# A new order of all steps and transfers in a one-core attention and gated-convolution kernel

## The chip, the cores and the metric

The kernel runs on one core of a Trainium2 chip. A core has five engines that run side by side, each through its own queue of instructions and strictly in the order of that queue as far as this kernel's rows show: PE (TensorE, matmuls; its weight loads are shown apart as PEld), DVE (VectorE), ACT (ScalarE), POOL (GpSimd) and SP (SyncE, which here only issues transfers). Matmul results land in PSUM; the other data lie in SBUF. POOL has no access to PSUM in this program: whatever it works on was first copied out by ACT or DVE. The metric is the device time of one execution in microseconds (us); lower is better.

## What is computed

Eight batches, eight heads, 576 rows. In each head the rows of k and v are first pooled into 32 slots with softmax weights made from phi, then each row of q attends to the 32 slots. The heads side by side are x (8, 576, 512), which goes through a causal convolution of five taps with a sigmoid (the gate) and through two matrix products:

```python
a = softmax(phi, axis=2)                        # per slot over the 576 rows
k_m = einsum('bhsm,bhsd->bhmd', a, k);  v_m = einsum('bhsm,bhsd->bhmd', a, v)
attn = softmax(q @ k_m.T / sqrt(64));   x = attn @ v_m      # heads side by side
gate_pre[:, s] = sum_k conv_w[k] * x[:, s - 4 + k]
out = (sigmoid(gate_pre) * (x @ w_val)) @ w_out
```

The weights arrive as float64 and are narrowed to float32 on the chip; the last products are made of a high and a low part each (three matmuls for one), so that they are exact enough.

## The kernel before

The program is cut into 900 small steps. A step is a function such as `project(k, i)`; its arguments are batch, half, group or tile. A string, `ORDER` (lines 41 to 143), names every step once, and a loop at the end calls them in that order. Each engine's queue is filled in the order in which the string reaches its instructions, so `ORDER` fixes the order on all five engines, the transfers on SP among them; semaphores between the engines follow from which step reads what another wrote. A star behind a name moves the step's work to its second engine (`pick(usual, other)`).

The steps of one batch, with the line by which the profile knows them:

- `load_phi`, `load_kv`, `load_rest`, `load_q` (L229 to L244) and, once, `load_w` (L258): transfers in, all issued by SP. The weights' transfers share two buffers (`hH`), so a later one waits until an earlier one was narrowed (`narrow_size` L267, `narrow_bits` L272, `narrow_round` L280, `narrow_add` L286, `narrow_done` L295, on ACT, DVE and POOL).
- `phi_max`, `phi_turn`, `phi_top`, `phi_spread`, `phi_sub` (L378: POOL, starred DVE), `phi_exp`: the first softmax.
- `slots` (PE L392, 40 matmuls in the trace), `slots_inv`, `slots_scale`, `slots_turn` (L422), `slots_place`, `scores` (PE L442), `scores_turn` (DVE L454), the `soft_...` steps (`soft_inv` begins on DVE L507, starred on ACT L505; `soft_high` is a copy, `soft_low` a subtraction).
- `val_rows` (PE L542) and `val_copy`, `val_high`, `val_low`: x @ w_val is made through the slots.
- the gate: for batch 0 `conv` (PE L580) and `sigmoid`; for the others `mix` (PE L593), which puts attn @ v_m into a PSUM tile `cv`, then five `tap` steps for each of two groups of channels. `tap.b.s.g.0` is on ACT: it reads `cv` and writes `gate` (two instructions, L615). Starred, it also writes the fifth tap into a tile `part` (two more of L615). Taps 1 to 4 are on DVE (two instructions each, L617, which read `cv` and `gate`); in a starred group the fifth is instead added by POOL from `part` (L609). `open_gate` is the sigmoid (ACT L622).
- `value` (PE L637), `gated` (DVE L650; starred a copy on ACT L648 and the product on POOL L650), `gated_high` (a copy, L209) and `gated_low` (a subtraction, L212: POOL, starred DVE).
- for each pair of batches, nine tiles of rows: `project` (PE L675, 12 matmuls), `place` (L209: PSUM to SBUF on ACT, starred on DVE), `store` (SP L685).

All copies have line L209 and all subtractions of low parts L212. PSUM holds two kinds of tiles: `b`, four buffers, shared by all small products, `value` and `project`; and `cv`, two buffers. `part` has one buffer. `warm` (PE L219) are matmuls whose result nobody reads.

```python
    def pick(usual, other):
        return other if live["other"] else usual
        ...
    with tc.manual_schedule():
        for x in ORDER.split():
            name, *args = x.rstrip("*").split(".")
            live["other"] = x.endswith("*")
            steps[name](*(int(a) if a.isdigit() else a for a in args))
```

Of the kernel before, what the change touches and what calls it, by code (L numbers as in the profile page):

```python
# [46 lines left out]
phi_lay.1 narrow_done.v.2 spread_taps.0 warm.2 narrow_bits.v.3 phi_exp.0.1 load_w.o.3 narrow_add.v.0 phi_sub.1*
slots_inv.0.0 narrow_done.v.0 slots_scale.0.0* narrow_add.v.3 slots.0.1 narrow_done.v.3 place_taps.0 load_rest.1
narrow_size.v.1 slots_inv.0.1 narrow_round.v.1 narrow_bits.v.1 slots_scale.0.1 narrow_add.v.1 slots_turn.0 taps.0.0*
narrow_done.v.1 spread_taps.1 phi_exp.1 slots_place.0 load_w.o.0 load_kv.1.1 scores.0 scores_turn.0.0 narrow_size.o.3  # L50
load_w.o.1 narrow_bits.o.3 soft_max.0.0 scores_turn.0.1 soft_sub.0.0* load_kv.1.0 place_taps.1 narrow_size.o.0
taps.0.1 val_rows.0 load_w.o.2 val_copy.0.1 soft_exp.0.0 soft_max.0.1 val_high.0.1 soft_sum.0.0 narrow_round.o.3
soft_inv.0.0 load_phi.2 warm.8 soft_sub.0.1 val_copy.0.0 soft_exp.0.1 val_high.0.0 soft_mul.0.0* narrow_round.o.0
slots.1.1 soft_turn.0.0 soft_high.0.0 slots_inv.1.1 turn_taps.0 soft_sum.0.1 narrow_add.o.3 conv.0.0 narrow_size.o.1
load_rest.2 narrow_done.o.3 sigmoid.0.0.1 sigmoid.0.0.0 narrow_size.o.2 soft_inv.0.1 soft_mul.0.1* val_low.0.1
narrow_round.o.1 soft_turn.0.1 narrow_bits.o.1 load_q.1 val_low.0.0 soft_low.0.0 slots.1.0 narrow_round.o.2
narrow_bits.o.0 narrow_bits.o.2 phi_max.2 conv.0.1 slots_scale.1.1* slots_inv.1.0 load_phi.3 soft_high.0.1 phi_turn.2
phi_top.2 narrow_add.o.1 value.0.0.1 narrow_done.o.1 narrow_add.o.2 slots_scale.1.0* sigmoid.0.1.0 lay_taps.0
phi_spread.2 slots_turn.1 phi_lay.2 slots_place.1 value.0.0.0 gated.0.0.1 load_kv.2.0 scores.1.0 sigmoid.0.1.1
scores.1.1 wo_high.1 narrow_add.o.0 val_rows.1 narrow_done.o.2 value.0.0.3 phi_sub.2 phi_exp.2 wo_high.3 val_copy.1.1  # L60
warm.2 gated.0.0.0 scores_turn.1.0 load_kv.2.1 scores_turn.1.1 wo_high.2 soft_max.1 gated.0.0.3 value.0.0.2
soft_low.0.1 soft_sub.1 phi_max.3 value.0.1.0 slots.2.0 gated.0.1.0 load_kv.3.0 narrow_done.o.0 phi_turn.3 wo_low.2
value.0.1.1 gated.0.0.2 slots_inv.2.0 val_copy.1.0 slots.2.1 soft_exp.1 gated_high.0.0.1 wo_low.1 value.0.1.2
soft_sum.1 gated_high.0.0.0 gated_low.0.0.1 phi_top.3 load_q.2 wo_low.3 gated.0.1.1 soft_inv.1* slots_scale.2.0*
phi_spread.3 slots_inv.2.1 wo_high.0 slots_scale.2.1* slots_turn.2 value.0.1.3 wo_low.0 soft_mul.1* load_phi.4
val_high.1.1 gated.0.1.2 phi_lay.3 soft_turn.1 slots_place.2 val_rows.2 gated_high.0.1.0 mix.1.1 gated_low.0.0.0
project.0.1 load_rest.3 phi_max.4 gated.0.1.3* project.0.0 val_high.1.0 val_low.1.1 tap.1.1.0.0 soft_high.1
tap.1.1.1.0* val_low.1.0 tap.1.1.0.1 tap.1.1.0.2 scores.2.0 tap.1.1.0.3 scores.2.1 soft_low.1 tap.1.1.1.1 tap.1.1.1.2
tap.1.1.1.3 gated_high.0.1.1 tap.1.1.1.4 tap.1.1.0.4 gated_low.0.1.1 scores_turn.2.0 scores_turn.2.1 value.1.1.3
val_copy.2.0 place.0.1 load_q.3 gated_low.0.1.0 soft_max.2 open_gate.1.1.0 mix.1.0 phi_turn.4 value.1.1.2 soft_sub.2  # L70
store.0.1 place.0.0 val_copy.2.1 value.1.1.1 load_kv.3.1 open_gate.1.1.1 tap.1.0.1.0* phi_sub.3 project.0.2
gated.1.1.3 tap.1.0.0.0 soft_exp.2 phi_top.4 gated.1.1.2 tap.1.0.1.1 place.0.2 phi_spread.4 load_phi.5 phi_exp.3
tap.1.0.1.2 project.0.3 val_high.2.1 value.1.0.2 tap.1.0.1.3 phi_lay.4 slots.3.0 tap.1.0.0.1 load_kv.4.0 soft_sum.2
soft_inv.2 tap.1.0.1.4 tap.1.0.0.2 place.0.3 tap.1.0.0.3 soft_mul.2 gated_high.1.1.1 tap.1.0.0.4 soft_turn.2 slots.3.1
mix.2.1 open_gate.1.0.1 tap.2.1.0.0 value.1.1.0 phi_sub.4 slots_inv.3.0 gated.1.1.1 load_rest.4 store.0.0 value.1.0.3
gated_low.1.1.1 slots_inv.3.1 gated.1.1.0* gated.1.0.2 value.1.0.0 slots_scale.3.0 slots_scale.3.1* load_kv.4.1
# [665 lines left out]
```

## Time and profile before

| | |
|---|---|
| time, median of 3 runs | 262.78 us (262.44 to 268.13) |
| the profiled execution's own time | 262.44 us |
| its span, first to last instruction | 260.6 us |
| time outside the span | 1.84 us (262.44 less 260.6) |
| granted TensorE clock, mean | 0.987 |
| bytes read and written | 37.92 MB and 9.44 MB |

The span is made of a head of some 40 us, in which data arrive and the weights are narrowed, a long middle in which PE, DVE, ACT and POOL work on several batches at once, and an end of some 15 us in which PE multiplies the last tiles by w_out. In the rows below a line is one group of instructions, with its busy time, the mean of one, and, behind the second bar or in brackets, how long the engine sat idle before them and what ended that.

### The profile page before, as it was taken

To read this page: it belongs to the slowest core of one execution; us is meant where nothing else is said; L and a number is where in the kernel's file an instruction comes from. 1 tells how busy PE (TensorE), PEld (TensorE's weight loads), DVE (VectorE), ACT (ScalarE), POOL (GpSimd) and SP (SyncE) were. 2 spreads that over 40 slices of the span, in tenths; PEclk is the share of its full clock that TensorE was granted. 3 is DMA by queue.
4 is the path that set the end of the run, shared out by engine and by line. 5 is a ranking of instruction groups with operands and counts; after the bars stand their busy time and mean duration, and the time that the engine had idled before them with its cause. 6 is when DMAs were issued, how large, how long until landed. Compare 5 with 4: busy or idle time off the path is not lost.

```text
span 260.6 us, 5969 instructions
## 1 busy us (share of the span) xinstructions
PE 234.0 (90%) x2344; PEld 180.2 (69%) x2344; DVE 214.7 (82%) x411; ACT 176.5 (68%) x328; POOL 181.8 (70%) x134
## 2 busy tenths in 40 slices
PE   1288889899999999999999999999987999999995
PEld 0255578574587777786868578866766587978884
DVE  2486898899999998899898999869679889799510
ACT  2454769877897978877878889477773595950402
POOL 2271485999999999877979799977495778840300
PEclk9999779999999999999999999999999999999999
DMA  6999995972191989803953009814501202122114
GB/s 187 402 358 334 401 396 155 394 291 89 21 361 50 384 282 346 298 9 123 390 221 121 3 3 337 330 42 114 190 3 40 76 11 111 53 80 82 40 47 154
DMA packets 12571, 47.73 MB, mean 183 GB/s; under 512 B 1400, under 2 KB 1656, under 8 KB 9600
## 3 DMA queue, kind: packets, MB, share of 16 engines
q1 hardware_dynamic: 12544, 47.36, 49.4%
q8 instruction: 18, 0.29, 0.5%
q14 instruction: 9, 0.07, 0.1%
HBM read 37.92 MB, written 9.44 MB: 182 GB/s over the span
## 4 chain that ended last, share of the span: by engine, by line
PE 34%; DVE 22%; DMA 14%; ACT 13%; POOL 11%; issue 4%; SPq 1%; ACTq 0%; DVEq 0%; POOLq 0%
PE b L675 17%; DVE gate L617 9%; PE b L637 8%; DMA out_dram<-o 8%; DMA hH<-in_w_val_dram 4%; ACT gate L615 3%; DMA hH<-in_w_out_dram 2%; PE cv L593 2%; POOL e L378 2%; POOL h L650 2%; PE cv L442 2%; POOL gate L609 2%; ACT part L615 2%; DVE ss L498 2%; PE b L392 2%
## 5 line engine op out<-in xcount | busy, mean ns | idle before, releaser
L617 DVE SCALAR_TENSOR_TENSOR gate<-cv,cwP,gate 128x288 f32<-128x288 f32 x202 | 88.6, 505 | 10.2 <-ACT part L615 6.2
L675 PE MATMUL b<-woH,hL 128*128 128x512 f32 (+1 forms) x148 | 58.1, 393 | 0.6 <-DVE ri L399 0.4
L675 PE MATMUL b<-woH,hH 128*128 128x512 f32 (+1 forms) x148 | 57.0, 385 | 0.0
L675 PE MATMUL b<-woL,hH 128*128 128x512 f32 (+1 forms) x148 | 56.8, 384 | 0.0
L650 POOL TENSOR_TENSOR h<-h,gate 128x288 f32<-128x288 f32 x30 | 26.8, 904 | 20.0 <-ACT h L648 14.8
L212 POOL TENSOR_TENSOR hL<-h,hH 128x576 fp32r<-128x576 f32 x25 | 35.6, 1429 | 5.8 <-ACT hH L209 4.3
L675 PEld LDWEIGHTS b<-woH,hL 128*128 128x128 f32 x148 | 27.8, 188 | 7.3 <-issue 1.6
L637 PE MATMUL b<-pL,vwH 128*128 128x288 f32 x128 | 29.7, 313 | 2.9 <-ACT vwF L209 1.2
L675 PEld LDWEIGHTS b<-woH,hH 128*128 128x128 f32 x148 | 27.8, 188 | 5.7
L675 PEld LDWEIGHTS b<-woL,hH 128*128 128x128 f32 x148 | 27.8, 188 | 4.9
L209 ACT COPY o<-b 128x512 f32<-128x512 f32 (+1 forms) x28 | 16.0, 579 | 21.1 <-PE b L675 21.0
L615 ACT ACTIVATE gate<-cv,cwP 128x288 f32<-128x288 f32 x56 | 24.6, 507 | 5.3 <-PE cv L593 4.9
L622 ACT ACTIVATE gate<-gate 128x576 f32<-128x576 f32 x28 | 19.1, 689 | 12.9 <-DVE gate L617 7.2
L637 PE MATMUL b<-pH,vwH 128*128 128x288 f32 x128 | 27.4, 295 | 0.0
L637 PE MATMUL b<-pH,vwL 128*128 128x288 f32 x128 | 27.3, 295 | 0.0
L637 PEld LDWEIGHTS b<-pL,vwH 128*128 128x128 f32 x128 | 20.5, 189 | 9.5 <-issue 3.5
L286 POOL TENSOR_TENSOR hL<-hL 128x512 int32<-128x512 int32 (+1 forms) x9 | 13.4, 1507 | 18.3 <-ACT hL L280 13.2
L209 ACT CAST hH<-h 128x576 fp32r<-128x576 f32 x26 | 17.6, 681 | 7.8 <-DVE h L650 4.6
L212 POOL TENSOR_TENSOR pL<-pT,pH 128x1152 fp32r<-128x1152 f32 (+1 forms) x9 | 22.5, 2501 | 0.0
L392 PE MATMUL b<-kv,e 128*32 128x129 f32 x512 | 19.3, 295 | 1.6 <-DMA kv<-in_kv_dram 1.3
L609 POOL TENSOR_TENSOR gate<-gate,part 128x576 f32<-128x576 f32 x11 | 16.3, 1478 | 6.1 <-DVE gate L617 4.9
L637 PEld LDWEIGHTS b<-pH,vwL 128*128 128x128 f32 x128 | 20.5, 188 | 0.0
(90 smaller groups left out, 466.7 us busy)
## 6 DMA issues: line engine op xcount, KB each, us to landing
kv<-in_kv_dram SPq DMA_DIRECT2D x16, 1032.0 KB, 9.1
out_dram<-o SPq DMA_DIRECT2D x35, 256.0 KB, 2.5
q<-in_q_dram SPq DMA_DIRECT2D x7, 1152.0 KB, 6.3
e<-in_phi_dram SPq DMA_DIRECT2D x7, 640.0 KB, 6.6
rest<-in_rest_dram SPq DMA_DIRECT2D x8, 258.0 KB, 7.9
...
```

The source lines that it names most:

```text
L209: eng.copy(out=out, in_=x) if eng is nc.scalar else eng.tensor_copy(out=out, in_=x)
L212: eng.tensor_tensor(out=out, in0=x, in1=hi.bitcast(F32), op=ALU.subtract)
L286: nc.gpsimd.tensor_tensor(out=a, in0=a, in1=r, op=ALU.add)
L378: eng.tensor_tensor(out=t, in0=t, in1=mxa.unsqueeze(3).to_broadcast(list(t.shape)), op=ALU.subtract)
L392: nc.tensor.matmul(km[j * M:(j + 1) * M, 0:2 * D + 1], lhsT=e[:, g, j * M:(j + 1) * M, c], rhs=x[:, c, j, :] if c < C - 1 else rests[b % 2 ...
L609: nc.gpsimd.tensor_tensor(out=gt, in0=gt, in1=part, op=ALU.add)
L615: nc.scalar.activation(out=o[:, t], in_=x, func=AF.Identity, scale=w)
L617: nc.vector.scalar_tensor_tensor(out=o[:, t], in0=x, scalar=w, in1=o[:, t], op0=ALU.mult, op1=ALU.add)
L622: nc.scalar.activation(out=gt, in_=gt, func=AF.Sigmoid)
L637: nc.tensor.matmul(vp[:, 0:HALF], lhsT=a[:, t // PG, n:n + P], rhs=p[:, g, s * HALF:(s + 1) * HALF], start=(i == 0), stop=(i == len(parts) ...
L650: eng.tensor_tensor(out=h[:, i], in0=x, in1=gt, op=ALU.mult)
L675: nc.tensor.matmul(ps, lhsT=h, rhs=w, start=(n == 0), stop=(n == len(parts) - 1))
```

## The change

`ORDER` is replaced. The same 900 steps stand in it, each once, in another sequence; nothing else of the kernel differs. A line of it before and one after, at the same place in the work (the first half of batch 5's gate):

```diff
-tap.5.1.1.4 tap.5.0.0.0* gated_low.4.1.1* project.2.0 val_low.5.1 value.5.1.0 tap.5.0.0.1 tap.5.0.0.2 open_gate.5.1.0
...
+phi_spread.7 value.5.1.0 gated.4.0.1* tap.5.1.0.3 gated_high.4.0.0 tap.5.1.1.4 tap.5.0.0.0 value.5.1.1 place.1.5*
+slots_place.6 gated_low.4.0.0 tap.5.0.1.0* load_q.6 tap.5.1.0.4 gated_low.4.1.1 project.2.0 scores.6.0 place.1.6*
+open_gate.5.1.0 tap.5.0.0.1 tap.5.0.0.2 val_rows.6 gated_low.4.1.0 tap.5.0.0.3 store.1.2 gated.5.1.1* scores.6.1
```

Stars differ too, so some work changes its engine. Counted over the string, DVE loses three `gated_low`, three `place`, one `phi_sub`, four first halves of `soft_inv` and one fifth tap, and gains two `soft_low`, one `soft_high` and one `taps`; one `gated` leaves it and one `gated_high` comes to it. POOL gains the three `gated_low`, the `phi_sub` and the fifth tap's addition and loses the two `soft_low`. ACT gains the three `place`, and its queue holds 18 loads of an activation table where it held 16.

The head, on PE. Rows of PE's queue from batch 0's slots (L392, from `kv` and `rest`) to its scores (L442); L302 spreads the convolution weights, L219 are the warming matmuls. Before:

```order
L392 MATMUL b<-kv_78,e 32x129 x16
L392 MATMUL b<-rest_81,e 32x129 x4
L302 MATMUL b<-taps,kvT 128x320
L219 MATMUL cv<-ident 128x128 x2
L392 MATMUL b<-kv_79,e 32x129 x16
L392 MATMUL b<-rest_81,e 32x129 x4
L422 MATMUL b<-ident,kvd 128x128 x3
L302 MATMUL b<-taps,kvT 128x320
L442 MATMUL cv<-q,kvT 32x288 x16
```

Of the change, on PE, from the same slots:

```order
L392 MATMUL b<-kv_78,e 32x129 x16
L392 MATMUL b<-rest_81,e 32x129 x4
L392 MATMUL b<-kv_79,e 32x129 x16
L392 MATMUL b<-rest_81,e 32x129 x4
L365 MATMUL b<-ident,top 128x128 x2
L422 MATMUL b<-ident,kvd 128x128 x3
L442 MATMUL cv<-q,kvT 32x288 x16
```

The second group's slots now follow the first's directly: the weight spreading and the warming matmuls went ahead of both. On SP, the transfer of `rest` now stands ahead of that of `kv_78`, not behind it.

The middle, on DVE. Rows of DVE's queue at the first half of batch 5: before, `gate_2245<-cv_2213` is the group whose first taps on ACT also write `part`, and `gate_2290<-cv_2214` the other; `hL_708` is a `gated_low`. Before:

```order
L212 TENSOR_TENSOR hL_708<-h_2128,hH_694 128x2x288
L617 SCALAR_TENSOR_TENSOR gate_2245<-cv_2213,cwP_84,gate_2245 128x288 x6
L209 COPY o_2334<-b_2252 128x512
L454 STREAM_TRANSPOSE st_2336<-cv_2281 128x576
L617 SCALAR_TENSOR_TENSOR gate_2290<-cv_2214,cwP_84,gate_2290 128x288 x2
```

Of the change, on DVE, at the same half; here `gate_2251<-cv_2202` is the group without `part`, and `gate_2266<-cv_2203` the one with it:

```order
L209 COPY o_2298<-b_2176 128x512
L617 SCALAR_TENSOR_TENSOR gate_2251<-cv_2202,cwP_84,gate_2251 128x288 x8
L650 TENSOR_TENSOR h_2319<-b_2237,gate_2169 128x288
L454 STREAM_TRANSPOSE st_2336<-cv_2289 128x576
L617 SCALAR_TENSOR_TENSOR gate_2266<-cv_2203,cwP_84,gate_2266 128x288 x2
L454 STREAM_TRANSPOSE st_2336<-cv_2322 128x576
```

DVE now takes the group without `part` first, all four of its taps, and comes to the group with `part` two steps after that.

The evictions, on ACT. Rows of ACT's queue where tiles of the first pair of batches leave PSUM (`o<-b` is a `place`); `e` is `phi_exp`, `st` is `soft_exp`, `gate<-gate` is `open_gate`. Before:

```order
L383 ACTIVATE e_743<-e_743 128x1280
L209 COPY o_1214<-b_1164 128x512
L209 CAST vwH_1232<-vwF_1184 128x512
L209 CAST hH_706<-h_1130 128x2x288
L492 ACTIVATE st_1162<-st_1162 128x1152
```

Of the change, on ACT, from the same `phi_exp` on; `b_1169` is `project.0.7`, which was the first of the three to be multiplied:

```order
L383 ACTIVATE e_652<-e_652 128x1280
L209 COPY o_1288<-b_1214 128x512
L209 COPY vwF_1290<-b_1142 128x512
L209 CAST vwH_1295<-vwF_1199 128x512
L492 ACTIVATE st_1184<-st_1184 128x1152
L615 ACTIVATE gate_1299<-cv_1270,cwP_84 128x288 x2
L411 ACTIVATE kvd_1285<-b_1248,ri_1292 128x128
L411 ACTIVATE kvd_1285<-b_1248,ri_1292 128x64
L622 ACT_TABLE_LOAD
L622 ACTIVATE gate_1077<-gate_1077 128x576
L209 COPY o_1361<-b_1317 128x512
L209 COPY o_1370<-b_1169 128x512
```

Tile 0.7 (`b_1164` before, `b_1169` now) left right behind the `phi_exp`; now 0.8 and 0.5 leave ahead of it, with a softmax, first taps, a table load and an `open_gate` between.

## Rows read from the trace of the kernel before

**Rows 1.** Page, busy time and share of the span of each engine.

```profile
PE 234.0 (90%) x2344; PEld 180.2 (69%) x2344; DVE 214.7 (82%) x411; ACT 176.5 (68%) x328; POOL 181.8 (70%) x134
```

**Rows 2.** Page, chain that ended last, share of the span by engine.

```profile
PE 34%; DVE 22%; DMA 14%; ACT 13%; POOL 11%; issue 4%; SPq 1%; ACTq 0%; DVEq 0%; POOLq 0%
```

**Rows 3.** Windows: busy us per engine, clock, DMA share, GB/s; the long middle.

```profile
60.00:240.00 180.00, 172.88 (x1629) 133.05 (x1629) 163.06 (x327) 134.08 (x250) 144.30 (x99) 1.00 0.41 147
```

**Rows 4.** Timeline of PE in the head: start, us, line, [idle <-releaser].

```profile
15.07 1.95 PE L392 MATMUL b<-kv,e 128*32 128x129 f32 x32 [0.20 <-DMA kv<-in_kv_dram]
...
17.38 1.43 PE L302 MATMUL b<-taps,kvT 8*128 8x320 f32 x2
...
19.90 1.95 PE L392 MATMUL b<-kv,e 128*32 128x129 f32 x32
...
34.83 4.48 PE L580 MATMUL cv<-pT,taps 32*64 32x288 f32 x80 [1.16 <-DVE ri L399]
```

**Rows 5.** Windows, the stretch in which the second `kv` arrives.

```profile
10.00:20.00 10.00, 7.59 (x60) 5.35 (x64) 7.93 (x15) 6.96 (x14) 6.64 (x4) 1.00 0.99 383
```

**Rows 6.** Page, issues of two transfers: count, KB each, median us to landing.

```profile
kv<-in_kv_dram SPq DMA_DIRECT2D x16, 1032.0 KB, 9.1
...
rest<-in_rest_dram SPq DMA_DIRECT2D x8, 258.0 KB, 7.9
```

**Rows 7.** Waits of DVE, 43 to 245 us: us in total, times, longest.

```profile
DVE gate L617 <- ACT part L615: 6.2, 5, 2.2
...
DVE gate L617 <- ACT gate L615: 3.7, 5, 1.6
```

**Rows 8.** Timeline of ACT, first half of batch 5's gate.

```profile
171.23 0.91 ACT L615 ACTIVATE gate<-cv,cwP 128x288 f32<-128x288 f32 x2
172.67 0.90 ACT L615 ACTIVATE part<-cv,cwP 128x288 f32<-128x288 f32 x2 [0.53 <-POOL gate L609]
```

**Rows 9.** Timeline of DVE at the same place.

```profile
173.60 2.64 DVE L617 SCALAR_TENSOR_TENSOR gate<-cv,cwP,gate 128x288 f32<-128x288 f32 x6 [2.24 <-ACT part L615]
```

**Rows 10.** Groups of DVE by form: count, busy us, mean ns.

```profile
L617 DVE SCALAR_TENSOR_TENSOR gate<-cv,cwP,gate 128x288 f32<-128x288 f32 x202 | 88.6, 505 | 10.2 <-ACT part L615 6.2 <-ACT gate L615 3.7
L212 DVE TENSOR_TENSOR hL<-h,hH 128x576 fp32r<-128x576 f32 x7 | 5.9, 849 | 0.8 <-ACT hH L209 0.7
L209 DVE COPY o<-b 128x512 f32<-128x512 f32 x8 | 5.5, 687 | 7.1 <-DMA out_dram<-o 3.8 <-PE b L675 3.1
L507 DVE TENSOR_SCALAR ss<-ss 128x36 f32<-128x36 f32 x6 | 3.7, 621 | 0.1
L378 DVE TENSOR_TENSOR e<-e,mxa 128x1280 f32<-128x1280 f32 x1 | 1.5, 1473 | 0.0
L209 DVE CAST pH<-pT 128x1152 fp32r<-128x1152 f32 x2 | 2.1, 1038 | 0.0
L567 DVE TENSOR_TENSOR taps<-h,kvd 128x320 f32<-128x320 f32 x1 | 1.4, 1412 | 0.0
L212 DVE TENSOR_TENSOR vwL<-vwF,vwH 128x512 fp32r<-128x512 f32 x2 | 4.4, 2214 | 0.0
```

**Rows 11.** Groups of POOL and ACT by form that the moved work joins or leaves.

```profile
L212 POOL TENSOR_TENSOR hL<-h,hH 128x576 fp32r<-128x576 f32 x25 | 35.6, 1429 | 5.8 <-ACT hH L209 4.3 <-DVE hH L209 1.4
L212 POOL TENSOR_TENSOR pL<-pT,pH 128x1152 fp32r<-128x1152 f32 x7 | 19.2, 2747 | 0.0
L609 POOL TENSOR_TENSOR gate<-gate,part 128x576 f32<-128x576 f32 x11 | 16.3, 1478 | 6.1 <-DVE gate L617 4.9 <-ACT gate L622 1.2
L378 POOL TENSOR_TENSOR e<-e,mxa 128x1280 f32<-128x1280 f32 x6 | 15.2, 2538 | 1.7 <-ACT mxa L209 1.7
L209 ACT COPY o<-b 128x512 f32<-128x512 f32 x27 | 15.6, 586 | 19.3 <-PE b L675 19.3
L622 ACT ACT_TABLE_LOAD x7 | 9.0, 1283 | 0.1
```

**Rows 12.** Waits of ACT, 43 to 245 us: us in total, times, longest.

```profile
ACT gate L622 <- POOL gate L609: 5.6, 1, 5.6
```

More of the change, by code (lines that the diff above doesn't have):

```diff
@@ L47 @@
[L47 to L76, printed above, removed]
@@ L137 @@
[L137 to L141 removed]
+load_w.c.0 load_phi.0.0 load_w.v.3 load_phi.0.1 narrow_size.c.0 narrow_round.v.3 narrow_round.c.0 phi_max.0.0
@@ new lines @@
+open_gate.1.0.0 value.1.0.0 slots_place.3 value.1.0.3 gated.1.0.1* gated_high.1.1.0 tap.2.1.0.4 gated_low.1.1.0
+gated.1.0.0 gated.1.0.2* store.0.2 tap.2.1.1.0* val_rows.3 gated.1.0.3* phi_sub.4 gated_high.1.0.0 phi_max.5
+scores.3.0 tap.2.1.1.1 project.0.7 store.0.3 gated_high.1.0.1 scores_turn.3.0 val_low.2.0 soft_high.2* scores.3.1
+val_copy.3.1 load_q.4 scores_turn.3.1 phi_turn.5 phi_exp.4 soft_max.3 phi_top.5 tap.2.1.1.2 project.0.8 slots.4.0
+slots.4.1 gated_low.1.0.1 mix.2.0 tap.2.1.1.3 slots_inv.4.0 slots_scale.4.0 place.0.8 val_copy.3.0 slots_inv.4.1
@@ new lines @@
+val_high.3.1 soft_sub.3 soft_exp.3 tap.2.0.0.0 soft_low.2* tap.2.0.0.1 load_kv.5.0 soft_sum.3 load_rest.5 phi_spread.5
+slots_scale.4.1* gated_low.1.0.0 open_gate.2.1.0 project.0.5 project.0.6 project.0.4 soft_inv.3 val_low.3.1
+tap.2.1.1.4 place.0.5 tap.2.0.0.2 load_phi.6 soft_mul.3 tap.2.0.0.3 place.0.7 load_kv.5.1 val_high.3.0 phi_lay.5
+tap.2.0.0.4 open_gate.2.1.1 tap.2.0.1.0* soft_turn.3 value.2.1.3 open_gate.2.0.0 phi_sub.5 store.0.5 place.0.6
+value.2.0.1 tap.2.0.1.1 value.2.0.0 tap.2.0.1.2 tap.2.0.1.3 phi_exp.5 gated.2.1.3 mix.3.1 slots.5.1 slots.5.0
@@ new lines @@
+tap.5.0.1.2 gated.5.0.0* tap.5.0.1.3 value.5.1.3 soft_sub.6 gated.5.1.2 soft_exp.6 gated.5.1.3 soft_sum.6 phi_exp.7
+project.2.2 value.5.0.3 soft_inv.6 slots.7.1 store.1.5 gated_high.5.1.1 soft_mul.6* soft_turn.6 slots_inv.7.1
+tap.5.0.1.4 open_gate.5.0.1 slots.7.0 mix.6.1 place.2.1 value.5.0.1 place.2.2 val_high.6.0 gated_low.5.1.0*
+val_low.6.1 tap.6.1.0.0 slots_inv.7.0 slots_scale.7.1* tap.6.1.1.0* store.1.4 load_q.7 gated.5.0.3* slots_scale.7.0
+soft_high.6 tap.6.1.0.1 value.5.0.2 tap.6.1.0.2 project.2.3 slots_turn.7 gated.5.0.1 gated_low.5.1.1* place.2.3
@@ new lines @@
+project.2.4 tap.6.0.0.2 gated.6.1.3 tap.6.0.0.3 store.2.1 project.2.8 soft_sum.7 tap.6.0.0.4 val_low.7.0 soft_inv.7
+gated_high.6.1.0 gated_high.6.1.1 place.2.8* tap.6.0.1.2 soft_mul.7 project.2.5 value.6.0.1 value.6.0.2
+gated_low.6.1.1 tap.6.0.1.3 gated_low.6.1.0 tap.6.0.1.4 project.2.6 place.2.4 soft_turn.7 open_gate.6.0.0 mix.7.0
+value.6.0.0 soft_high.7* gated.6.0.1 val_low.7.1 soft_low.7* open_gate.6.0.1 gated.6.0.2* tap.7.0.0.0 place.2.6*
+gated.6.0.0* tap.7.0.0.1 value.6.0.3 tap.7.0.0.2 store.2.3 tap.7.0.1.0* project.3.3 store.2.7 gated_high.6.0.0
```

145 lines of the change are left out of this document (76 added, 69 removed).

## Prediction

> **What bounds the kernel now.** I read the page's busy shares first [rows 1]: PE is busy 90% of the 260.6 us, DVE 82%, POOL 70%, ACT 68%. No engine stands far apart, so a single bound is not to be expected. The chain that ended last says the same [rows 2]: followed back from the end it runs 34% of the span through PE, 22% through DVE, 14% through transfers, 13% through ACT and 11% through POOL. The windows then show where PE has room [rows 3]: between 60 and 240 us it is busy 172.88 of 180 us, which leaves 7.1 us, while DVE is busy 163.06 and so idles 16.9 us, ACT 45.9, POOL 35.7. The rest of PE's idle time lies in the head. So an order can gain in two ways: by making the head shorter, and by taking from the middle waits that keep PE from work. The work itself hardly changes: the matmuls are the same in number.
>
> Next come DVE's own waits in the middle [rows 7]. The largest is for ACT's first taps: 6.2 us in five waits behind the writing of `part`, and 3.7 us in five behind the writing of `gate`. What such a wait is shows in batch 5 [rows 8, 9]. ACT has written `gate` by 172.14 (171.23 + 0.91), which is all of ACT's data that DVE's second tap reads. It then waits 0.53 us for POOL to give back the one `part` buffer and writes `part` until 173.57. DVE starts at 173.60, 0.03 us behind that, though it reads no `part`, and had been idle for 2.24 us. What the two share is the PSUM tile `cv`: DVE's read of it does not begin before ACT's last read ends. The Trainium skill, page "PSUM — Partial Sum Buffer", section "PSUM bank collisions raise a hardware error", says that two engines must not touch one bank in the same partitions at once, two reads included, and that software has to keep them apart; the trace agrees by that 0.03 us. By that rule the wait cannot be removed, only covered with other DVE work, and so I price it.
>
> **The change part by part.**
>
> *Head.* Before, the second group's slots began at 19.90, with the weight spreading (17.38) and then the warming matmuls between them and the first group's [rows 4]. The change puts those two ahead of both groups, where PE waited for data anyway. What is late next is the transfer. The first `kv` had landed at about 15.07 [rows 4]. Behind it come, in either order, `rest` (258 KB) and the second `kv` (1032 KB) [rows 6]: 1290 KB at the 383 GB/s of that stretch [rows 5] are 3.4 us, so 18.4. The first group itself is 0.7 us later, because `rest` (258 KB by the same rate) now lands ahead of its `kv`: 15.8, and with its 2.3 us (17.38 less 15.07) it ends at 18.1, ahead of that transfer. So the second group begins at 18.4 where it began at 19.90, and scores, softmax and the first convolution (34.83, [rows 4]), which hang on it, can follow 1.5 us earlier. Ends: nothing, if ACT, which now has the narrowing of w_out ahead of the first softmax's exponential, waits for that transfer as long as before; and -2.5, if the transfer is no limit and the second group simply loses what stood between (17.38 to 19.90). I take **-1.5**, because the transfer's rate has a row and the wait on w_out depends on a buffer that the change frees earlier.
>
> *Cover for the first taps.* For each group of taps, the DVE steps that stand in the string between ACT's first tap and DVE's second are its cover, and I add them up by the means of DVE's groups (a tap is two L617 of 505 ns, 1.0 us) [rows 10]. A starred group needs 1.8 us of cover (0.91 + 0.90) [rows 8], another 0.9. Of the starred groups 3 of 11 are covered before and 7 of 12 after; what lacks falls from 9.9 us to 4.7. Of the others 9 of 17 are covered before and 10 of 16 after; what lacks goes from 5.4 to 6.2. If the measured waits [rows 7] follow what lacks, the waits behind `part` go from 6.2 to 6.2 x 4.7/9.9 = 2.9, and those behind `gate` from 3.7 to 3.7 x 6.2/5.4 = 4.2. Batch 5's first half, worked in the rows above, is one of those now covered: DVE does the whole group without `part` first. Sum **-2.7**. Ends: nothing, if other waits step in (what is late next on DVE is the `gated` products, which wait for `open_gate` and `value`); -6.2, if all waits behind `part` go. DVE's waits count in full here, because each delays the gates, the `gated` steps and with them `project`; the cover if that is false is PE's queue of ready `project` tiles, and that is the second rival.
>
> *Work that changes its engine* [rows 10, 11]. Off DVE: three `gated_low` at 0.849 (2.5), three `place` at 0.687 (2.1), one `phi_sub` 1.47, four first halves of `soft_inv` at 0.621 (2.5), one fifth tap of two L617 (1.0): 9.6 us. Onto DVE: `soft_high` 1.04, `taps` 1.41, and two `soft_low`, a form that DVE has no row for. Its nearest row is `gated_low` on DVE, the same subtraction of half the size: twice 0.849 is 1.7 each. The farther one is `val_low` on DVE, 2.214 for 512 elements, which for 1152 would be 5.0 each. I take 1.7, the row nearest in operands and count. So 5.9 come and the net is -3.7 (upper end: 12.4 come, net +2.8). The Trainium skill, page "SBUF — State Buffer", section "Who interferes with whom", states that a DVE instruction with two SBUF inputs contends with GpSimd's reads; both rows are of that kind, the slow one agrees and the fast one does not show it, and by that rule the sum would use 5.0 each and be 1.4 us longer (6.6 more on DVE, times the share below). POOL gains 3 x 1.429 + 2.538 + 1.478 and loses 2 x 2.747: +2.8. ACT gains three `place` at 0.586 and two table loads at 1.283: +4.4. `gated` and `gated_high`, one each way, are left out. How much of it lies on the path? I weigh it by each engine's share of the chain [rows 2]: -3.7 x 0.22 = -0.8, +2.8 x 0.11 = +0.3, +4.4 x 0.13 = +0.6. Sum **+0.1**, ends -3.7 (DVE sets the pace alone) and +2.8 (POOL does, or DVE with the dear `soft_low`). What hides the rest is that ACT and POOL idle a fifth to a quarter of the middle [rows 3].
>
> *The end* is priced at nothing: after the last `value` PE has the same five tiles to multiply in both strings, one copy and one store follow, and DVE's and POOL's last gates are covered by tiles that need only earlier halves.
>
> Sum: -1.5 - 2.7 + 0.1 = -4.1. The profiled execution took 262.44 us, 0.1% under the median of 262.78, so both scales give the same answer: **258.3 us**. The bounds add up to -2.5 - 6.2 - 3.7 = -12.4 and +2.8, so 250.0 to 265.2.
>
> **The rivals.**
>
> *Everything in the middle loosens.* The other sequence could also save the many small waits of PE that no single row explains. The limit is PE's room: 7.1 us in the middle [rows 3] and up to 2.5 in the head, -9.6: 252.8 (250 to 255.5). For it speaks that DVE's work falls by 3.7 us; against it, that ACT and POOL get more and that the two strings have PE's steps in nearly the same sequence.
>
> *PE has no room.* At 96% busy in the middle [rows 3], a DVE wait that goes may only let finished values lie longer in PSUM. Then only the head counts: 262.4 - 1.5 = 260.9 (259.5 to 262.5). For it: PE's longest shares of the chain are `project`. Against: PE's busy time is modelled, so some of the 172.88 is slack.
>
> *Slower: PSUM is held by results that nobody fetches.* The place is where tiles 0.7, 0.8, 0.5, 0.6 and 0.4 are multiplied. Before, DVE evicted two of the five; now ACT evicts all five, and 0.7 stands behind 0.8 and 0.5 with a softmax, first taps and a table load ahead of it. For all that time one of four `b` buffers is taken, and PE, which is in order, stops at the next product that needs one. Price: the longest stop that ACT shows in front of such work is 5.6 us [rows 12]; two of them in full on PE are +11.2, less the gain of 4.1: 269.5 (263 to 270). It decides from 9.4 us of such stops on (5.3 us is 2% of the median, and 4.1 is gained first). For it: ACT is the engine with the extra table loads. Against: PE has `mix`, `value` and `slots` of the next batch between, and ACT idles 25% of the middle.
>
> **How the numbers follow.** The sum as worked out: 0.44, with its own range of 255 to 261, in which two fifths lie below 257.5, 2% under the median (about what a measurement of this kernel can tell from no change). Everything loosens: 0.22, all of it below 257.5. PE has no room: 0.20. Slower: 0.14, of which 0.10 above 268.0. So faster by over 2%: 0.22 + 0.18 = 0.40; slower 0.10; the same 0.50. The range from 252 to 265 leaves out about half of the second case, 0.1, and most of the last, 0.1.
>
> **What the profile of the changed kernel would show.** The head is right if the second group's slots begin near 18.4 and the first matmul of `conv` near 33.3. The cover is right if DVE's waits behind `part` sum to about 3 us and those behind `gate` to about 4. The moves are right if DVE's busy time is near 211 and each `soft_low` on DVE takes about 1.7. The prediction is wrong if PE shows waits of over 2 us for ACT's copies near tiles 0.7 to 0.4, if the first convolution begins no earlier, or if DVE's lost waits come back under other names, `gated` for `open_gate` above all.

## The result, and the profile after

The changed kernel takes 255.17 us (median of four executions, 254.88 to 256.14) against 263.5 for the kernel before (262.44 to 268.13): a ratio of 0.970, with an interval of 0.965 to 0.976. That is 3.0% faster, 7.9 us. The profiled execution took 254.88 us and its span is 253.1 us, 7.5 us shorter than before. The kernel before scatters from one execution to the next (260.6 to 268.9 us in the later comparisons), so the intervals below are wide, and the ratios leave out executions that ran longer as a whole, one of 757.7 us of the run with seven copies on ACT among them.

The first lines of the page of the changed kernel are its busy times and its chain by engine; they answer to [rows 1] and [rows 2].

```profile
PE 230.7 (91%) x2344; PEld 177.4 (70%) x2344; DVE 217.1 (86%) x402; ACT 181.7 (72%) x338; POOL 184.0 (73%) x137
...
PE 43%; DVE 32%; POOL 9%; ACT 5%; DMA 4%; issue 4%; SPq 1%; DVEq 0%; POOLq 0%; ACTq 0%
```

DVE is busy 217.1 us where it was busy 214.7. The prediction had 211. The span nevertheless fell by 7.5 us, so DVE's idle time fell by 9.9 us (45.9 to 36.0). Transfers and ACT have nearly left the chain (14% to 4% and 13% to 5%).

The next two views split the middle at 150 us, which [rows 3] and [rows 7] did not. First the windows of the kernel before and then of the one after (columns: window, its length, busy time of PE, PEld, DVE, ACT and POOL with instructions, granted clock, DMA share, GB/s).

```profile
60.00:150.00 90.00, 87.39 (x948) 65.03 (x951) 85.10 (x169) 74.83 (x135) 80.02 (x55) 1.00 0.52 190
150.00:235.00 85.00, 80.49 (x671) 63.87 (x662) 73.01 (x148) 58.66 (x114) 64.28 (x45) 1.00 0.30 106
```

```profile
60.00:150.00 90.00, 89.11 (x963) 69.39 (x964) 86.00 (x171) 78.95 (x147) 84.95 (x58) 1.00 0.58 213
150.00:235.00 85.00, 82.63 (x652) 65.47 (x650) 79.60 (x152) 57.38 (x109) 58.76 (x42) 1.00 0.25 91
```

Then DVE's waits from 150 to 235 us, before and after (columns: who waited for whom, us in total, times, longest).

```profile
DVE gate L617 <- ACT part L615: 5.0, 3, 2.2
DVE gate L617 <- ACT gate L615: 2.8, 2, 1.6
DVE o L209 <- DMA out_dram<-o: 2.0, 1, 2.0
DVE hH L209 <- POOL h L650: 1.1, 1, 1.1
DVE st L454 <- PE cv L442: 0.3, 1, 0.3
```

```profile
DVE st L454 <- PE cv L442: 2.2, 2, 1.6
DVE gate L617 <- ACT gate L615: 1.7, 2, 1.1
DVE h L650 <- PE b L637: 0.4, 1, 0.4
DVE ss L498 <- ACT st L492: 0.2, 1, 0.2
DVE gate L617 <- ACT part L615: 0.2, 1, 0.2
```

Most of the old waits stood here: of the 9.9 us behind ACT's first taps in [rows 7], 7.8 lie between 150 and 235 us. In the same stretch 1.9 us are left, and DVE idles 5.4 of 85 us where it idled 12.0. From 60 to 150 us DVE was already busy 85.1 of 90 us and gained 0.9.

Where the time was won can be followed on PE at `mix`, the step that opens half a batch. These are the starts of mix.3.1, 5.1, 6.1 and 7.1, first before, then after (start us, us, engine, line, operation, tile).

```profile
109.29 1.26 PE L593 MATMUL cv<-pT,kvd 32*64 32x292 f32 x16
160.91 0.75 PE L593 MATMUL cv<-pT,kvd 32*64 32x292 f32 x16
192.03 0.75 PE L593 MATMUL cv<-pT,kvd 32*64 32x292 f32 x16 [0.83 <-DVE ri L399]
228.50 0.72 PE L593 MATMUL cv<-pT,kvd 32*64 32x292 f32 x8
```

```profile
106.76 0.75 PE L593 MATMUL cv<-pT,kvd 32*64 32x292 f32 x16
156.23 0.75 PE L593 MATMUL cv<-pT,kvd 32*64 32x292 f32 x16 [0.27 <-DVE pT L520]
186.68 0.75 PE L593 MATMUL cv<-pT,kvd 32*64 32x292 f32 x16
223.41 0.94 PE L593 MATMUL cv<-pT,kvd 32*64 32x292 f32 x16
```

The lead is 2.5 us at 107, 4.7 at 156, 5.3 at 187 and 5.1 at 223; at the end it is 7.5. Such a lead can be compared only where the same work stands ahead of the step in both strings. That holds for PE at mix.5.1 and mix.6.1. Ahead of mix.3.1 the new string has one `value` more, ahead of mix.7.1 two more (0.8 us of PE each), so in work the lead is 3.3 us at 107 and 6.7 at 223. These windows run from mix.5.1 to the end, before and after (columns as above).

```profile
160.91:260.60 99.69, 92.36 (x691) 73.64 (x690) 73.14 (x145) 54.28 (x104) 56.43 (x40) 1.00 0.27 97
```

```profile
156.23:253.10 96.87, 91.85 (x690) 73.08 (x690) 74.98 (x141) 58.12 (x108) 57.64 (x41) 1.00 0.26 94
```

For this last part, with the same work on PE, the kernel before needs 99.7 us and the changed one 96.9. So 2.8 of the 7.5 us were won in it, though all of the late waits behind ACT's first taps lie there (7.8 us before, 1.9 after), and 4.7 us ahead of it. Each trace is a single execution.

The head, third. These are PE's rows for the slots of batch 0 and the first convolution; they answer to [rows 4].

```profile
14.75 1.96 PE L392 MATMUL b<-kv,e 128*32 128x129 f32 x32 [0.41 <-DMA kv<-in_kv_dram]
16.45 0.69 PE L392 MATMUL b<-rest,e 128*32 128x129 f32 x8
17.23 1.57 PE L392 MATMUL b<-kv,e 128*32 128x129 f32 x32
...
33.32 0.50 PE L580 MATMUL cv<-pT,taps 32*64 32x288 f32 x8 [1.81 <-DVE pT L520]
```

The second group's slots follow the first at once, at 17.23 instead of 19.90, and show no wait for their transfer. The first convolution begins at 33.32, 1.5 us earlier than in [rows 4]; the second, conv.0.1, ends 2.9 us earlier (40.36 for 43.28).

### The profile page after: what moved, and what is told of

The parts are those of the page before. It is cut to its first block, busy times and chain, and to the rows that moved or that the text cites. A ratio compares the mean times of both kernels' runs of the same rounds, so it can differ in the third digit from the quotient of the medians.

```text
span 253.1 us, 5959 instructions
## 1 busy us (share of the span) xinstructions
PE 230.7 (91%) x2344; PEld 177.4 (70%) x2344; DVE 217.1 (86%) x402; ACT 181.7 (72%) x338; POOL 184.0 (73%) x137
## 4 chain that ended last, share of the span: by engine, by line
PE 43%; DVE 32%; POOL 9%; ACT 5%; DMA 4%; issue 4%; SPq 1%; DVEq 0%; POOLq 0%; ACTq 0%
PE b L675 22%; DVE gate L617 12%; PE b L637 12%; PE b L392 3%; DMA e<-in_phi_dram 3%; POOL hL L212 3%; PE cv L442 3%; PE cv L593 2%; DVE pT L520 2%; DVE ss L498 2%; DVE hH L209 2%; POOL woL L212 2%; PE b L542 1%; DVE hL L295 1%; DMA hH<-in_w_val_dram 1%
## 5 line engine op out<-in xcount | busy, mean ns | idle before, releaser
L617 DVE SCALAR_TENSOR_TENSOR gate<-cv,cwP,gate 128x288 f32<-128x288 f32 x200 | 87.7, 505 | 2.7 <-ACT gate L615 2.0
L212 POOL TENSOR_TENSOR hL<-h,hH 128x576 fp32r<-128x576 f32 x28 | 41.2, 1485 | 4.7 <-ACT hH L209 2.2
L209 ACT COPY o<-b 128x512 f32<-128x512 f32 (+1 forms) x31 | 17.6, 580 | 17.3 <-PE b L675 13.0
L286 POOL TENSOR_TENSOR hL<-hL 128x512 int32<-128x512 int32 (+1 forms) x9 | 12.2, 1365 | 17.1 <-ACT hL L280 9.2
L209 ACT CAST hH<-h 128x576 fp32r<-128x576 f32 x25 | 16.6, 680 | 8.8 <-POOL h L650 5.0
L212 POOL TENSOR_TENSOR vwL<-vwF,vwH 128x512 fp32r<-128x512 f32 x14 | 20.8, 1491 | 1.5 <-ACT vwH L209 1.5
L637 PEld LDWEIGHTS b<-pH,vwH 128*128 128x128 f32 x128 | 20.5, 188 | 0.0
L609 POOL TENSOR_TENSOR gate<-gate,part 128x576 f32<-128x576 f32 x12 | 17.5, 1461 | 3.1 <-DVE gate L617 3.1
```

Source lines behind the costliest of these rows:

```text
L209: eng.copy(out=out, in_=x) if eng is nc.scalar else eng.tensor_copy(out=out, in_=x)
L212: eng.tensor_tensor(out=out, in0=x, in1=hi.bitcast(F32), op=ALU.subtract)
L286: nc.gpsimd.tensor_tensor(out=a, in0=a, in1=r, op=ALU.add)
L609: nc.gpsimd.tensor_tensor(out=gt, in0=gt, in1=part, op=ALU.add)
L617: nc.vector.scalar_tensor_tensor(out=o[:, t], in0=x, scalar=w, in1=o[:, t], op0=ALU.mult, op1=ALU.add)
L637: nc.tensor.matmul(vp[:, 0:HALF], lhsT=a[:, t // PG, n:n + P], rhs=p[:, g, s * HALF:(s + 1) * HALF], start=(i == 0), stop=(i == len(parts) ...
```

## The experiments

**The two halves of the order.** The strings of before and after agree closely enough that a first part of one can be followed by the rest of the other, with each step once and its star from the part that it comes from. Four kernels were made so.

```diff
 h1_after_head:   steps 1-135 of after (to narrow_round.o.2, 40 us), then the rest as before
 h2_after_to_100: steps 1-345 of after (to load_q.4, 95 us),         then the rest as before
 l1_after_late:   steps 1-344 of before (to soft_high.2, 95 us),     then the rest as after
 l2_after_late:   steps 1-255 of before (to phi_turn.4, 63 us),      then the rest as after
```

> The order of the changed kernel up to the step narrow_round.o.2 (its first 135 steps, to the end of the first convolution), and behind it all other steps in the order of the kernel before. The two traces place the end of conv.0.1 at 40.36 us after and 43.28 us before. Theory 'head': these 2.9 us are gained once and kept, so 262.8 - 2.9 = 259.9 us (259 to 261). My own term for the head was -1.5, which would be 261.3. Rival 'slack': the middle of the kernel before waits for other things anyway and swallows the earlier start: 262.5 or more.

Measured: 260.93 us, ratio 0.9935 (0.988 to 0.999), which is -1.7 us with an interval of -0.3 to -3.1. The profiled span is 257.5 us, 3.1 under that of before. The head's gain is there alone and is kept. The point agrees with the -1.5 of the prediction; the interval does not exclude the 2.9 of the traces.

> The order of the changed kernel up to the step load_q.4 (its first 345 steps, to about 95 us), and behind it all other steps in the order of the kernel before. In the traces project.1.0 ends 3.4 us earlier after than before (at about 130 us), and the tiles from batch 5 on gain about 4 us more. Theory 'two separate gains': the second gain comes from the order of the late steps themselves, so this kernel has only the first: 262.8 - 3.2 = 259.6 us (259 to 260.5), and no faster than the kernel with the head alone by more than 0.7. Rival 'early gain shown late': what runs before 100 us sets up the late gain, and this kernel comes to 255 to 257.

Measured: 261.44 us, ratio 0.9948 (0.991 to 0.999), -1.4 us: over the range that it was given (259 to 260.5), but no faster than the kernel with the head alone, as the theory said. As far as 95 us the trace leads before by 2.8 us, but at the seam 1.6 us are lost, which belongs to the cut and not to either order: at 98.7 us the sum of the softmax of batch 3 waits for its exponential, where neither the kernel before nor the changed one waits. The row is from DVE's waits of this kernel.

```profile
DVE ss L498 <- ACT st L492: 1.6, 1, 1.6
```

So the second gain is not prepared before 95 us.

> The order of the kernel before up to the step soft_high.2 (its first 344 steps, to about 95 us), and behind it all other steps in the order of the changed kernel: the counterpart of the run with the early order alone, which came to 0.9948 of before, 1.4 us. Theory 'late cover': DVE's waits of batches 5 to 7 (in the trace of before 0.98 at 163.5 us, 2.24 at 173.6, 1.61 at 194.9, 1.19 at 209.9 and 1.75 at 223.4, together 7.8 us) go by the late order alone, so nearly all of the rest, 7.9 - 1.4 = 6.5 us, is found here: a ratio of 0.975 (0.972 to 0.980), about 257 us. Rival 'the two halves need each other': 0.985 or more, 259 us and up.

> The order of the kernel before up to its 255th step (phi_turn.4, about 63 us) and behind it all other steps in the order of the changed kernel: once more the late order alone, with the seam at another place than in the run that was cut at 95 us (ratio 0.986). In the traces the changed kernel is 2.4 to 2.7 us ahead at that place (project.0.1, mix.1.0), and 7.2 at the end. Theory 'two separate gains': 7.9 - 2.5 = 5.4 us are found here, a ratio of 0.980 (0.976 to 0.984), 257 to 258 us. Rival 'the halves need each other': 0.987 or more.

Measured: 0.9864 (0.979 to 0.994) and 0.983 (0.975 to 0.991), that is -3.6 and -4.5 us. The first misses its forecast of 0.975 and lies where its rival was put (0.985 or more); the second meets its own of 0.980 within its interval. In the second, DVE's waits from 150 to 235 us are those of the changed kernel, row by row (part 0.2, gate 1.7, st 2.2). With the head's 1.7 to 3.1 us that accounts for 5.3 to 7.6 of the 7.9: two gains, one in the first 40 us and one in the late order. Where the second lies, PE's row for mix.5.1 of the second kernel shows.

```profile
161.28 0.75 PE L593 MATMUL cv<-pT,kvd 32*64 32x292 f32 x16 [0.27 <-DVE pT L520]
```

It begins no earlier than before (160.91). From there to the end of its span (258.1 us) it needs 96.8 us, as the changed kernel does. By the traces the late order is then worth 2.9 us, which the ratio's interval (2.3 to 6.7 us) does not exclude.

**Cover taken away.**

```diff
 (after, seven starred groups; on DVE alone)
-tap.5.1.0.0* store.1.8 ... tap.5.1.1.2 tap.5.1.1.3 tap.5.1.0.1
+tap.5.1.0.0* tap.5.1.0.1 store.1.8 ... tap.5.1.1.2 tap.5.1.1.3
```

> The changed kernel with one thing undone on DVE alone: in the seven starred groups of taps whose wait is covered by other DVE work (1.1.1, 3.1.1, 5.1.0, 5.0.1, 6.1.1, 6.0.0, 7.0.1) DVE's second tap is moved directly behind ACT's first, so that nothing covers the wait. Lacking cover rises by 7 x 1.8 = 12.6 us; with the factor of the trace before (6.2 us of wait for 9.9 lacking) DVE's waits behind part rise by 7.9 us. Theory 'cover counts in full': 255.2 + 7.9 = 263 us (260 to 265). Rival 'slack': the DVE work that is pushed back has room behind it, the waits appear on DVE but the time stays within 255 to 256.5; then the late gain has another cause.

Measured: 268.38 us, 13.2 us over the changed kernel, above the range that it was given (260 to 265) and slower than before too (1.020, 1.009 to 1.030). DVE's waits of this kernel show the cause.

```profile
DVE gate L617 <- ACT part L615: 12.2, 5, 3.2
...
DVE gate L617 <- ACT gate L615: 1.6, 2, 1.2
```

The waits behind `part` rose from 0.7 to 12.2 us and the span from 253.1 to 265.7: 11.5 us of wait, 12.6 of time. The delay was not absorbed anywhere. The size was above the expected 7.9, since I had scaled it by 6.2/9.9; cover that is taken away counted nearly once (11.5 of 12.6), not by two thirds. Nor did it count only late in the kernel. Two of the seven groups lie before 150 us, and the first of them waited in full.

```profile
61.10 0.94 DVE L617 SCALAR_TENSOR_TENSOR gate<-cv,cwP,gate 128x288 f32<-128x288 f32 x2 [2.85 <-ACT part L615]
```

The other waited 0.7 us at most; of the five behind 150 us three waited 2.7 to 3.2 us each.

**A piece of the change undone.**

```diff
-tap.5.1.1.0  ... tap.5.1.0.0*    (and 5.0.0/5.0.1*, 7.0.0/7.0.1*)
+tap.5.1.1.0* ... tap.5.1.0.0
```

> The changed kernel with one piece of the change undone: in three pairs of tap groups (5.1, 5.0, 7.0) the group with two accumulators is again the first of the pair, as in the kernel before (5.1.1, 5.0.0, 7.0.0 starred, 5.1.0, 5.0.1, 7.0.1 not). By the string, cover lacks 0.9 us more at 5.1.1, 0.4 at 5.0.0 and 0.9 at 7.0.0, 2.2 together. Theory 'cover counts in full, late in the kernel' (the run with seven groups uncovered lost 13.2 us for 12.6 us of lacking cover): 255.2 + 2.3 = 257.5 (256.5 to 258.5). Rival 'only the sequence of PE counts': 255.2, within 0.5.

Measured: 260.91 us, ratio to before 0.9929 (0.989 to 0.997), so 5.7 us over the changed kernel and above the range that it was given (256.5 to 258.5). Not all of that is the cover. By PE's rows it falls back in three steps, and mix.6.1 starts at 191.73 instead of 186.68. The first 0.8 us stand at mix.5.1 already (157.06 for 156.23), ahead of all that the edit touches: a copy on DVE, gated_high.3.0.0, took longer in this execution (first the changed kernel, then this one).

```profile
145.23 1.54 DVE L209 CAST hH<-h 128x576 fp32r<-128x576 f32 x1
```

```profile
145.29 2.32 DVE L209 CAST hH<-h 128x576 fp32r<-128x576 f32 x1
```

From there to the end of tile 2.0 (175.3 for 173.2) 1.3 us more are lost, as much as was forecast for the groups 5.1.1 and 5.0.0 (0.9 and 0.4). The last 2.9 us are lost behind that. At 7.0, where 0.9 was forecast, nothing is lost. The waits of PE (150 to 235 us) and of ACT (180 to 192 us) in this kernel name the last step.

```profile
PE b L392 <- ACT o L209: 2.7, 1, 2.7
```

```profile
ACT gate L622 <- DVE gate L617: 2.9, 1, 2.9
```

Without its star, the fifth tap of group 5.0.1 falls to DVE, at a place in the string that was chosen for POOL. ACT's `open_gate` waits 2.9 us for it, two `place` stand behind that on ACT, their tiles hold PSUM, and the `slots` of batch 7 wait 2.7 us for a buffer. This part is a product of my edit (the fifth tap was not moved), but it shows the rival of the held PSUM at work.

**Work moved between engines.**

```diff
 m1: -gated_high.1.1.1* 2.0.0* 2.0.1* 3.0.0* 4.0.1* 4.1.0* 7.0.1*  soft_high.2* 3*   (star off: ACT)
 p1: -soft_low.2* soft_low.7* val_low.5.1*                                           (star off: POOL)
 m2: -place.1.1* 1.5* 1.6* 2.6* 2.8*  val_copy.5.0* 6.0*                             (star off: ACT)
```

> The changed kernel with nine copies from SBUF to SBUF taken off DVE and given to ACT at the same places (gated_high.1.1.1, 2.0.0, 2.0.1, 3.0.0, 4.0.1, 4.1.0, 7.0.1, soft_high.2 and 3). In its trace they take 11.8 us of DVE in all (0.46 to 1.75 us each), against 0.45 us for the same gated_high in the trace of before where no POOL instruction ran beside it. Theory 'DVE sets the pace': DVE's time counts in full, less what new waits take: 255.2 - 11.8 = 243.4, at best, 245 to 249 with some waits. Rival 'ACT is late instead': the seven halves at 0.7 us and two at 1.2 us on ACT (7.3 us) push back first taps and sigmoids behind them, and DVE and POOL wait for those: 253 to 258 us.

Measured: 255.0 us, ratio 0.973 (0.968 to 0.977): no change, within the range of the rival. The page's busy times of this kernel are these.

```profile
PE 228.3 (90%) x2344; PEld 177.4 (70%) x2344; DVE 205.4 (81%) x393; ACT 186.8 (74%) x347; POOL 182.1 (72%) x137
```

DVE lost 11.7 us of work and the kernel gained nothing: waits for ACT's first taps came back instead (gate 2.0 to 6.6 us, part 0.7 to 2.0). "DVE sets the pace" falls as a statement about busy time that is moved to ACT. It does not follow that DVE's time is worth nothing. This is PE's row for mix.5.1 in this kernel.

```profile
158.32 0.75 PE L593 MATMUL cv<-pT,kvd 32*64 32x292 f32 x16
```

There it is 2.1 us behind the changed kernel (156.23), and at mix.6.1 it is level (186.90 for 186.68). From the one to the other it needs 28.6 us, the changed kernel 30.5. So in a stretch with two copies less on DVE (3.1 us in the changed kernel) it won 1.9 us, after the waits for ACT had cost as much ahead of it.

> The changed kernel with three subtractions moved from DVE back to POOL (soft_low.2, soft_low.7, val_low.5.1). In its trace they take 1.97, 2.07 and 1.33 us on DVE; my term for the moves had 1.7 for each soft_low. On POOL they cost about 2.7, 2.7 and 1.3 us. Theory 'DVE sets the pace': 255.2 - 5.4 = 249.8 (250 to 253). Rival 'POOL is late instead': pL and vwL come later, value and with it the gated products wait, and the kernel is as fast or slower: 255 to 260 us; then moving soft_low to DVE was worth its price.

> The changed kernel with seven copies out of PSUM moved from DVE to ACT (place.1.1, 1.5, 1.6, 2.6, 2.8, val_copy.5.0, 6.0). In its trace each takes 0.63 to 0.69 us on DVE whether POOL runs beside it or not, 4.7 us in all; on ACT about 0.6 each, 4.1 us. Theory 'DVE sets the pace': 255.2 - 4.7 = 250.5 (250.5 to 253). Rival 'ACT is late instead', or PSUM is given back later: 255 to 258 us.

Measured: 256.44 us (0.976, 0.969 to 0.983) and 256.4 (0.978, 0.973 to 0.982). Both lie where their rivals were put. They are 1.2 us over the changed kernel, which the scatter of the first (254.82 to 257.39) does not tell from none, although DVE has 4.7 us less to do in it. What the new order put on DVE is at least not dear in time.

**What bounds the changed kernel.**

```diff
-KVS = 3
+KVS, LESS = 3, {(1, 4), (1, 5), (1, 6), *((2, i) for i in range(NT))}
 ...
-for h, w in (("hL", woH), ("hH", woL), ("hH", woH))]
+for h, w in (("hL", woH), ("hH", woL), ("hH", woH)) if w is not woL or (k, i) not in LESS]
```

> Leaves work out: in twelve of the 36 output tiles (1.4 to 1.6 and 2.0 to 2.8, all multiplied between 150 and 235 us) the four matmuls with woL are not made, 48 matmuls of 0.385 us, 18.5 us of PE. Otherwise the changed kernel. It asks what bounds the changed kernel between 150 and 235 us, where PE is busy 82.6 and DVE 79.6 of 85 us. Theory 'PE': the copies taken off DVE (11.8 us) gained nothing because PE sets the pace; with PE relieved the time falls until DVE's own 5.4 us of idle time are used up: 249 to 251. Rival 'neither alone': DVE follows so closely that the time falls by less than 2 us: 253 to 255.

> Leaves out the same 48 matmuls of project, and has the nine copies on ACT instead of DVE as well. Theory 'PE first, DVE close behind': with both relieved the kernel falls further than with PE relieved alone, by about the 4.7 us that the three copies after 150 us (4.0.1, 4.1.0, 7.0.1) took on DVE: 2 to 5 us under the run with PE alone, 245 to 248. Rival 'the chain of gates through ACT and POOL sets the pace once PE does not': no more than 1 us under it.

Measured: 256.61 us (0.976, 0.967 to 0.984) and 254.48 (0.969, 0.962 to 0.976). The first lies above both of its forecasts. The second is 2.1 us under the first, as its theory said, but not at 245 to 248, and 0.7 us under the changed kernel, with times that overlap. In the first, mix.6.1 starts at 186.84, where the changed kernel had 186.68, though six of the twelve shortened tiles lie ahead of it. PE simply waited more. The windows of this kernel show that, and a second effect.

```profile
150.00:200.00 50.00, 42.90 (x417) 32.03 (x416) 46.12 (x90) 35.44 (x70) 36.95 (x26) 0.97 0.34 122
200.00:235.00 35.00, 31.68 (x181) 26.09 (x180) 31.70 (x60) 20.01 (x37) 21.28 (x16) 0.90 0.11 42
```

PE was busy 42.9 of 50 us and waited the rest. Behind that its granted clock is 0.90 on average between 200 and 235 us, where the changed kernel has 1.00, which means a part of that stretch at the lower of its two levels, 1.2 GHz. mix.6.0 still starts level with the changed kernel (197.88 against 197.95), mix.7.1 starts 1.8 us later (225.25 against 223.41). So PE's busy time does not set the pace between 150 and 200 us.

The second kernel, with DVE relieved too, is 1.1 us ahead at mix.6.1 (185.62).

```profile
158.13 0.75 PE L593 MATMUL cv<-pT,kvd 32*64 32x292 f32 x16
```

By this row it needs 27.5 us from mix.5.1 to mix.6.1, against 30.5 in the changed kernel, 30.9 in the first run and 28.6 with the copies on ACT alone. So DVE's work counts in that stretch, but here too ACT's delay had cost 1.9 us by mix.5.1. At mix.7.0 it leads by 2.5 us (211.22 against 213.77) and at mix.7.1 it is level (223.57); its clock between 200 and 235 us is 0.90 as well. How much of that lead the clock took was not tested, nor which steps of ACT and POOL the chain runs through at its tightest.

**The clock in the head.**

```diff
+warm.4
 slots.1.1 ...
+warm.4
 conv.0.0
```

> The kernel before with two further groups of eight warming matmuls (warm.4: 128x128, results unused), one ahead of slots.1.1 and one ahead of conv.0.0, both in gaps in which PE waits (30.18 to 31.29 and 33.67 to 34.83 us). In the trace of before the granted clock stands at half from 34 to about 40 us and conv.0.0 takes 4.48 us; after, it is full there and conv.0.0 takes 2.69 us. Theory 'clock': with the gaps filled the clock stays full, conv.0.0 takes about 2.7 us, and the kernel gains up to 1.8 us: 261.0 (260.5 to 261.8); then about 1.8 of the 2.9 us of the head is the clock and not the earlier start. Rival 'not on the path' or the clock falls all the same: 262.8, or up to 1 us longer for the warming itself.

Measured: 262.63 us, ratio 0.9994 (0.9935 to 1.0053). Its profiled execution took 267.95 us, so only the head is read from it. There the clock did what was meant: its window from 20 to 45 us shows 1.00 where before had 0.86.

```profile
20.00:45.00 25.00, 23.69 (x399) 16.88 (x392) 20.15 (x35) 16.35 (x31) 13.15 (x10) 1.00 0.90 345
```

PE's time in the two convolutions of batch 0 fell from 7.24 to 5.57 us. But the added warming pushed the first from 34.83 to 35.87, so it ended only 0.6 us earlier (38.7 for 39.3), and the second, behind a wait of 0.7 us, ended at 43.4 as before (43.3). These are the two rows.

```profile
35.87 2.88 PE L580 MATMUL cv<-pT,taps 32*64 32x288 f32 x80
...
40.66 2.69 PE L580 MATMUL cv<-pT,taps 32*64 32x288 f32 x80 [0.66 <-ACT hL L267]
```

The second convolution waits for ACT there and begins no earlier than in the kernel before (40.52), though the first ends earlier. So in the order of before the low clock costs the head next to nothing. A gain of 1.7 us is at the edge of the interval, so the total alone would settle little. Whether the clock has a part in the gain of the new order is another question, and the run with the head alone leaves it open: its own low clock lies from 22 to 30 us, and both of its convolutions run at the full one.

```profile
33.05 2.69 PE L580 MATMUL cv<-pT,taps 32*64 32x288 f32 x80 [0.88 <-DVE pT L520]
...
37.48 2.69 PE L580 MATMUL cv<-pT,taps 32*64 32x288 f32 x80 [0.48 <-ACT kvd L411]
```

Of the 3.1 us by which it ends conv.0.1 earlier than before (40.2 for 43.3), 1.8 stand at the start of conv.0.0 (33.05 for 34.83) and are not the clock of the convolutions. The other 1.3 can be that clock or the new order of ACT's steps.

## Why the prediction was right or wrong

The time lay within the range (252 to 265), but not where the prediction put it: 258.3 was 3.1 us too slow, "the same" was called likelier (0.50) than "faster" (0.40), and 255.17 lies at the very edge of the sum's own range (255 to 261) and just inside that of the rival "everything loosens". (The two scales do not quite give the same answer, as the prediction says: from the median of 262.78 the sum comes to 258.7.) In the traces the 7.5 us are 2.9 by the end of conv.0.1, 1.8 from there to mix.5.1 and 2.8 behind it; the prediction had 1.5 for the head and 2.6 for all the rest. Which of the two was short by more is not settled, since the run with the head alone gave 1.7 us by its median and 3.1 by its trace.

*Head, -1.5.* Right in size by its own run (-1.7, -0.3 to -3.1), and conv began where it was put (33.3), but in part by luck. A step of it failed: the second group was put at 18.4 because its transfer was thought to be next. It began at 17.23 with no wait, 2.7 us earlier than before and not 1.5, and 1.2 us of that were lost on the way to conv, which waited 1.81 us for DVE's `pT`. `rest` ahead of `kv` was to cost the first group 0.7 us, and it began 0.3 us earlier (14.75 against 15.07).

*Cover, -2.7.* Right that lacking cover shows as waits of DVE and that DVE's other work can cover them; wrong in the size of the waits, and not shown in what they are worth. The step that failed: "If the measured waits [rows 7] follow what lacks, the waits behind `part` go from 6.2 to 6.2 x 4.7/9.9". That is one factor for the whole kernel. The measured waits were 0.7 behind `part` and 2.0 behind `gate`, -7.2 in all. The windows say why. Until 150 us DVE is busy 95% and mostly comes late to the taps anyway, so lacking cover (8.5 us in batches 1 to 4 before) showed only 2.1 us of wait. From 150 us on DVE has room, and 6.9 us of lacking cover showed 7.8 of wait. The change takes the lacking cover of batches 5 to 7 from 6.9 to 1.2 us and lets that of batches 1 to 4 rise from 8.5 to 9.7. Priced by stage, the late waits would have come to 7.8 x 1.2/6.9 = 1.4 us, where 1.9 were measured.

"DVE's waits count in full here" is not shown for waits that go. From mix.5.1 to the end 5.9 us of wait behind the first taps went and 2.8 us of time, 2.9 in the run with the late order alone. DVE had 1.8 us more to do in that stretch (74.98 for 73.14), and other waits came in. So -6.4 in the place of -2.7 would bring the sum to 254.6, but that this is near the measured time is luck. What counted in full is wait that was added: in the run that uncovered seven groups, 12.6 us of time for 11.5 of wait, and in the part of the run with three pairs that its edit explains, 1.3 us.

*Work that changes its engine, +0.1.* The term was not measured alone; its working was wrong. DVE's busy time was to fall by 3.7 us and rose by 2.4. Each `soft_low` took 2.02 us (1.7 taken, 5.0 the other end). ACT's +4.4 leaves out the four first halves of `soft_inv` that come to it (0.34 us each); its busy time rose by 5.2. Most of the rest on DVE is the copies that the prediction left out as "one each way". The rows are from DVE's groups by form, first before, then after.

```profile
L209 DVE CAST hH<-h 128x576 fp32r<-128x576 f32 x6 | 2.7, 447 | 1.2 <-POOL h L650 1.1
L209 DVE CAST pH<-pT 128x1152 fp32r<-128x1152 f32 x2 | 2.1, 1038 | 0.0
```

```profile
L209 DVE CAST hH<-h 128x576 fp32r<-128x576 f32 x7 | 8.5, 1215 | 0.2
L209 DVE CAST pH<-pT 128x1152 fp32r<-128x1152 f32 x3 | 5.2, 1728 | 0.0
...
L212 DVE TENSOR_TENSOR pL<-pT,pH 128x1152 fp32r<-128x1152 f32 x2 | 4.0, 2019 | 0.0
```

The same copy of a half costs 0.447 us on average before and 1.215 after: 5.8 us more for one copy more. Whether a share of the chain is the right weight is not shown. The run with nine such copies on ACT gained nothing for 11.7 us less on DVE, but there ACT's delay took back what DVE's relief had won.

*The end, 0.* Nearly right. The lead is 5.1 us at mix.7.1 (223 us) and 7.5 at the end, but 1.6 of these 2.4 us are the two `value` steps that the new string has ahead of mix.7.1 and the old one behind it. What gives the other 0.8 was not tested alone.

*The rivals.* "Everything loosens" gave the nearest time. PE's idle time in [rows 3] went from 7.1 to 3.4 us, half of the way to its limit; but what was to speak for it, 3.7 us less work on DVE, was false, and a part of the gain has rows, the large late waits of DVE. "PE has no room" is refuted: with half of the 18.5 us of PE's work left out ahead of it, mix.6.1 starts no earlier. "PSUM held by results that nobody fetches" did not come about at tiles 0.7 to 0.4 (no wait of PE's in the changed kernel for ACT's copies above 1 us), but the run with three pairs undone brought it about by 2.7 us, one step from the string as it stands. DVE's lost waits did not come back as `gated` for `open_gate`. Between 150 and 235 us 1.9 us came back as `scores_turn` waiting for PE's scores, and at 238 us one `gated_low` waits 3.0 us for ACT's `gated_high`, where the kernel before has 0.7: the prediction's sign of lost waits under other names came true in part.
